# Paired norm transposes, one store per tile, smaller V and q arrays, and a new plan for the front of a two-layer attention and gated-MLP kernel

## The chip, the cores and the metric

The kernel runs on one core of a Trainium2 chip. The metric is device time in microseconds (us) from the first to the last instruction of the core, as the median of several runs. The core has a matmul engine (TensorE, PE in the profile), two engines for elementwise work (VectorE or DVE, ScalarE or ACT), GpSimd (POOL), and SyncE (SP), which here only issues DMAs.

## The reference

Two layers follow each other, with the same weights in both. Each is a sliding-window attention and then a gated MLP, both on a normalised x and both added to x. Everything is bf16; x has 2048 rows of 512.

```python
def _A_ref(x, wqkv, wo):
    H = 32; Dh = D // H; W = 256                      # 32 heads of 16
    q, k, v = ...                                     # x @ wqkv, split
    scores = einsum("bhqd,bhkd->bhqk", q, k) * (Dh ** -0.5)
    mask = (i - j >= 0) & (i - j < W)                 # 256 keys back
    p = softmax(where(mask, scores, -1e9))
    return einsum("bhqk,bhkd->bhqd", p, v) ... @ wo

def _B_ref(x, w_gate, w_up, w_down):                  # 512 -> 1792 -> 512
    return (sigmoid(x @ w_gate) * (x @ w_up)) @ w_down

x = x + _A_ref(_layernorm(x), wqkv, wo)
x = x + _B_ref(_layernorm(x), w_gate, w_up, w_down)
x = x + _A_ref(_layernorm(x), wqkv, wo)
x = x + _B_ref(_layernorm(x), w_gate, w_up, w_down)
```

## The kernel before

The 2048 rows are 16 tiles of 128, in four groups of four. The kernel's Python holds a plan: a small model of the chip (`Plan`) in which engines, queues and transfers have durations. While the program is built, the plan walks through time and decides at each step which unit of matmul work comes next; the other engines take tasks by priority. So the order of every engine's instructions is fixed before the kernel runs, by the plan's constants. Work of the MLP (gate, up, down) fills PE between pieces of attention: scores ("visits", 154 of them, each with one exponential on ScalarE) and values (P times V).

Layer norm of one tile: statistics on VectorE, the root on GpSimd, normalising on VectorE, and then a transpose, since the matmuls need the transposed tile `xnT`. The first eight tiles of layer 0 and two others are transposed by PE, all others by DMA, a tile at a time:

```python
def stats(e):
    nc.vector.bn_stats(out=st[:, 0:6], in_=self.xsb[:, t, :])
    nc.vector.bn_aggr(out=st[:, 6:8], in_=st[:, 0:6])
def root(e):
    nc.gpsimd.tensor_scalar(...); nc.gpsimd.tensor_tensor(..., op=ALU.pow)
def apply(e):                      # takes one of 3 xn buffers
    nc.vector.tensor_scalar(out=b[0][:], in0=self.xsb[:, t, :], ...)

a = pl.task({"DVE": 910}, stats, deps, prio, lambda: self.has("st"))
b = pl.task({"POOL": 800}, root, [a.done], prio)
c = pl.task({"DVE": 406}, apply, [b.done], prio, can, port=True)
if key[:2] == ("p", 0) and t < 8 or key[0] == "g" and self.by_pe(key[1], t):
    ...                            # nc.tensor.transpose x4, then a copy
else:
    d = pl.dma(1210, 131072, lambda: nc.sync.dma_start_transpose(
        out=self.xnT[key][0][:, :, o:o + P], in_=box["xn"][0][:]), [c.done], prio)
```

Buffers, the stores at the end of layer 1, the loads and the warm-up:

```python
self.qT = big.tile([P, NCQ, S], BF16, name="qT")
self.Vaug = [big.tile([P, NBG, VW], BF16, name=f"Vaug{i}") for i in range(3)]   # NBG = 4 tiles each
ring("xn", 3, [P, D]); ring("xnT", 3, [P, KT, TGW]); ring("st", 6, [P, 10], F32)
...
dst = self.out[0, t * P:(t + 1) * P, :].rearrange("(z k) d -> z k d", z=2)
for z in range(2):
    pl.dma(450, HP * D * 2, lambda z=z: nc.sync.dma_start(out=dst[z], in_=self.xsb[z:P:2, t, :]), [d.done])
...
for i in range(0, FC, 2):          # loads of w_down, after wq, wo, gate and up
    parts.append(load(self.wd[:, h, :], wd_src[:, h, :], 2 * P * D * 2, after=at))
    at += gap
...
def matmul(self, mode, ns):        # in the plan
    if self.now < COLD:            # COLD = 13600
        ns *= 2
...
def keep_warm(self, bank):         # when PE would have nothing to do, before 85 us
    for i in range(4):
        nc.tensor.matmul(self.banks[bank][:, 0:P], lhsT=self.ident[:], rhs=self.ident[:], start=True, stop=True)
```

Attention's result goes through two further DMA transposes per tile (OTs to Oq, On to OnT), and halves of V are copied by DMA (Vaug to Vl and Vh). All of these, the norm transposes and the stores are issued by SyncE, in one order.

Of the kernel before, what the change touches and what calls it, by code (L numbers as in the profile page):

```python
# [10 lines left out]
ALU = mybir.AluOpType  # L11
# [18 lines left out]
HP = P // 2  # L30

# [65 lines left out]
PACE = (2700, 3100)  # L97
OVERLAP = {"ACT": 114, "DVE": 83, "POOL": 45, "SP": 0}
LATENCY = {"ACT": 45, "DVE": 40, "POOL": 60, "SP": 0}
EXTRA = {"ACT": 40, "DVE": 10, "POOL": 30, "SP": 70}  # L100
PE_LATENCY = 180
COLD = 13600
SWITCH = 96
DMA_LATENCY = 1500
FETCH = (1200, 1300)
# [62 lines left out]
class Plan:  # L168
# [3 lines left out]
    def __init__(self):  # L172
        self.now = 0.0
        self.heap = []
        self.seq = 0
        self.free = {e: 0.0 for e in OVERLAP}
        self.queue = {e: [] for e in OVERLAP}
        self.mode = None
        self.pe_free = 0.0
        self.dma_free = 0.0  # L180
        self.issued = 0
        self.fetched = -1e9
        self.port_free = 0.0
# [18 lines left out]
    def dispatch(self):  # L202
        moved = True
        while moved:
            moved = False
            for e in ("ACT", "DVE", "POOL", "SP"):
# [4 lines left out]
                for t in q:  # L211
                    if t.port and self.port_free > self.now + 50:
                        continue
                    if not t.began and (t.can is None or t.can()) and (best is None or (t.prio, t.seq) < (best.prio, best.seq)):
                        if len(t.engines) > 1 and self.elsewhere(t, e):
                            continue
                        best = t
# [11 lines left out]
    def begin(self, t, e):  # L229
# [9 lines left out]
        if t.transfer:  # L239
            t.ends = max(t.ends, self.dma_free) + DMA_LATENCY  # L240
            self.at(t.ends, lambda: self.land(t, self.free[e] - 300))
        else:
            self.at(t.ends, t.done.fire)

    def land(self, t, since):

        if self.fetched >= since - FETCH[0]:
            self.at(self.fetched + FETCH[0] + FETCH[1], t.done.fire)
        else:
            t.done.fire()  # L250

    def count(self, n):

        if (self.issued + 2 * n) // 256 > self.issued // 256:
            self.fetched = self.now
            if self.free["SP"] > self.now:
                self.free["SP"] += 900
                self.at(self.free["SP"])
        self.issued += 2 * n

    def dma(self, ns, nbytes, fn, deps=(), prio=5, after=0, queue="SP"):
        def go(e):
            fn()
            self.dma_free = max(self.dma_free, self.now + ns) + nbytes / 250.0

        t = self.task({queue: ns}, go, deps, prio, None, after)
        t.transfer = True
        return t
# [14 lines left out]
    def matmul(self, mode, ns):  # L283
# [3 lines left out]
        if self.mode != mode:  # L287
            ns += SWITCH
            self.mode = mode
        self.pe_free = self.now + ns  # L290
# [8 lines left out]
class Net:  # L299


    def __init__(self, ctx, tc, A_x, wqkv, wo, w_gate, w_up, w_down, out):
# [22 lines left out]
        self.qT = big.tile([P, NCQ, S], BF16, name="qT")  # L325
        self.kTp = [big.tile([P, NCQ, NBG, 2, P], BF16, name=f"kTp{i}") for i in range(2)]
        self.Vaug = [big.tile([P, NBG, VW], BF16, name=f"Vaug{i}") for i in range(3)]
# [10 lines left out]
        self.nhalf = big.tile([P, 1], F32, name="nhalf")  # L338
        self.rms = [big.tile([P, 1], F32, name=f"rm{e}") for e in range(2)]
        self.bufs = {}  # L340

# [3 lines left out]
        ring("xn", 3, [P, D])  # L345
        ring("xnT", 3, [P, KT, TGW])
# [7 lines left out]
        ring("st", 6, [P, 10], F32)  # L354
# [19 lines left out]
    def loads(self, A_x, wqkv, wo, w_gate, w_up, w_down):  # L374
# [8 lines left out]
        def load_x(dst, tiles, n, prio, queues=("SP", "SP"), after=0):  # L383
            done, parts = Event(), []
            for z in range(2):
                src = A_x[0].rearrange("(t z k) d -> z k t d", z=2, k=HP)[z][:, tiles, :]
                parts.append(load(dst[z:P:2], src, n * HP * D * 2, after, (), prio, queues[z]))
# [3 lines left out]
        def load(dst, src, nbytes, after=0, deps=(), prio=2, queue="SP"):  # L391
            ns = max(520, 40 + nbytes / 1024 * 0.95)
            q = {"SP": nc.sync, "ACT": nc.scalar}[queue]
            return pl.dma(ns, nbytes, lambda: q.dma_start(out=dst, in_=src), deps, prio, after, queue).done
# [3 lines left out]
        for i, k in enumerate("kqv"):  # L398
            h = slice("qkv".index(k) * D, ("qkv".index(k) + 1) * D)
            self.has_wq[k] = load(self.wq[:, :, h], wq_src[:, :, h], D * D * 2, prio=0, queue="ACT" if i < 3 else "SP")  # L400

        def x_group(g, after):
            h = slice(g * NBG, (g + 1) * NBG)
            ev = load_x(self.xsb[:, h, :], h, NBG, 2 if g > 1 else 2, after=after)
            for t in range(g * NBG, (g + 1) * NBG):
                self.has_x[t] = ev

        x_group(1, 0)
        gap, at = 1600, 6000
        self.has_wo = load(self.wot[:], wo_src, D * D * 2, after=at)  # L410
        at += gap * 2
        n = F // 2
        gu = []
        for i in range(2):
            h = slice(i * n, (i + 1) * n)
            pair = []
            for w, src in ((self.wg, wg_src), (self.wu, wu_src)):
                pair.append(load(w[:, :, h], src[:, :, h], D * n * 2, after=at))
                at += gap * 7 // 2
            gu.append(pair)  # L420
            if i == 0:
                x_group(2, at)
                at += gap * 2
        self.has_gu = [gu[fc * 2 // FC] for fc in range(FC)]
        self.has_wd = Event()
        parts = []
        for i in range(0, FC, 2):
            h = slice(i, i + 2)
            parts.append(load(self.wd[:, h, :], wd_src[:, h, :], 2 * P * D * 2, after=at))
            at += gap  # L430
        when_all(parts, self.has_wd.fire)
        x_group(3, at)

    def constants(self):
# [4 lines left out]
                                base=0, pattern=[[-1, P]], channel_multiplier=1)  # L439
        nc.vector.memset(self.rms[0][:], 0.0)  # L440
# [4 lines left out]
        n = VS * H // 2  # L445
        for z in range(2):
            eng = nc.vector if z == 0 else nc.gpsimd
            for V in self.Vd[z]:
                eng.memset(V[0:HP, :, n:VW], 0.0)
                eng.memset(V[HP:P, :, 0:n], 0.0)  # L450
                eng.memset(V[HP:P, :, 2 * n:VW], 0.0)
        for V in self.Vaug:
            nc.vector.memset(V[:, :, 0:VS * H].rearrange("p t (h c) -> p t h c", c=VS)[:, :, :, 16:VS], 1.0)
            nc.vector.memset(V[:, :, VS * H:VW], 0.0)
        self.pl.free["POOL"] = 4000.0
# [3 lines left out]
        self.pl.free["DVE"] = 3200.0  # L459

    def later_constants(self):
        nc, pl = self.nc, self.pl

# [20 lines left out]
        a = pl.task({"POOL": 900}, mask, prio=7, port=True)  # L484
# [4 lines left out]
    def layer_norm(self, key, t, deps, prio):  # L489

        nc, pl = self.nc, self.pl
        done = self.xn_ready[key, t]
        box = {}

        def stats(e):
            box["st"] = b = self.take("st")
            st = b[0]
# [3 lines left out]
        def root(e):  # L501
            st = box["st"][0]
            nc.gpsimd.tensor_scalar(out=st[:, 9:10], in0=st[:, 7:8], scalar1=1e-5, scalar2=None, op0=ALU.add)  # L503
            nc.gpsimd.tensor_tensor(out=st[:, 8:9], in0=st[:, 9:10], in1=self.nhalf[:], op=ALU.pow)  # L504
# [10 lines left out]
        def apply(e):  # L515
            box["xn"] = b = self.take("xn")
            if key not in self.xnT:
                self.xnT[key] = self.take("xnT")
            st = box["st"][0]
            nc.vector.tensor_scalar(out=b[0][:], in0=self.xsb[:, t, :], scalar1=st[:, 6:7], scalar2=st[:, 8:9],  # L520
                                    op0=ALU.subtract, op1=ALU.mult)

        a = pl.task({"DVE": 910}, stats, deps, prio, lambda: self.has("st"))
        b = pl.task({"POOL": 800}, root, [a.done], prio)
        c = pl.task({"DVE": 406}, apply, [b.done], prio, can, port=True)
        c.done.then(lambda: self.give(box["st"]))
        o = (t % NBG) * P
        if key[:2] == ("p", 0) and t < 8 or key[0] == "g" and self.by_pe(key[1], t):
            def steps(bank):
                pt = self.tp_view(bank)  # L530
                xn = box["xn"][0]
# [3 lines left out]
            def evac(u):  # L535
                pt = self.tp_view(u.bank)
                d = pl.task({"ACT": act_ns(KT * P), "DVE": dve_ns(KT * P) + 100}, lambda e: self.copy(
                    e, self.xnT[key][0][:, :, o:o + P], pt), [u.done], 0 if t < NBG else 2)
# [4 lines left out]
        else:  # L543
            d = pl.dma(1210, 131072, lambda: nc.sync.dma_start_transpose(
                out=self.xnT[key][0][:, :, o:o + P], in_=box["xn"][0][:]), [c.done], prio)
            d.done.then(lambda: (self.give(box["xn"]), done.fire()))
# [11 lines left out]

    def used(self, key, n):
# [4 lines left out]
    def q_unit(self, L, g, cq):  # L564
        nc, pl, key = self.nc, self.pl, ("p", L, g)
        t0 = g * NBG

        by_tile = L == g == 0 and cq < 1
        w = P if by_tile else TGW

        def steps(bank):
            return [(mm_ns(w), lambda kt=kt, o=o: nc.tensor.matmul(  # L572
                self.banks[bank][:, o:o + w], lhsT=self.wq[:, kt, cq * P:cq * P + P], rhs=self.xnT[key][0][:, kt, o:o + w],
                start=kt == 0, stop=kt == KT - 1)) for o in range(0, TGW, w) for kt in range(KT)]

        def evac(u):
            u.done.then(lambda: self.used(key, 1))
            d = pl.task({"ACT": act_ns(TGW), "DVE": dve_ns(TGW)}, lambda e: self.copy(
                e, self.qT[:, cq, t0 * P:t0 * P + TGW].rearrange("p (t z k) -> p t z k", z=2, k=HP),
                self.banks[u.bank][:].rearrange("p (t k z) -> p t z k", z=2, k=HP)), [u.done], 3)  # L580
# [5 lines left out]
        if L == 1:  # L586
            needs.append(self.seen[0, t0 + NBG - 1])
# [5 lines left out]
    def k_unit(self, L, g, cq):  # L593
# [3 lines left out]
        by_tile = L == g == 0 and cq < 1  # L597
        w = P if by_tile else TGW

        def steps(bank):  # L600
            return [(mm_ns(w), lambda kt=kt, o=o: nc.tensor.matmul(  # L601
                self.banks[bank][:, o:o + w], lhsT=self.wq[:, kt, D + cq * P:D + cq * P + P], rhs=self.xnT[key][0][:, kt, o:o + w],
                start=kt == 0, stop=kt == KT - 1)) for o in range(0, TGW, w) for kt in range(KT)]

        def evac(u):
# [12 lines left out]
            a = pl.task({"ACT": act_ns(TGW), "DVE": dve_ns(TGW)}, cp, [u.done], 3, lambda: self.has("kt"))  # L618
            b = pl.task({"DVE": 620}, split, [a.done], 3, port=True)
# [726 lines left out]
```

The softmax here doesn't subtract the row's maximum and nothing guards it: scores larger than these inputs give would overflow.

## Time and profile before

| | |
|---|---|
| median of 3 runs | 551.94 us (550.83 to 552.82) |
| span of the profiled run | 551.2 us |
| TensorE busy | 527.5 us |
| VectorE busy | 414.5 us |
| ScalarE busy | 395.5 us, of which the 154 exponentials 282.6 |
| GpSimd busy | 63.1 us |
| mean granted clock of TensorE | 0.997 |
| DMA packets | 97,015, 36.41 MB |

In the profile an instruction is named by line, engine and "out<-in". L532 is the transpose by PE, L544 the norm's transpose by DMA, L572, L601 and L637 the projections to q, k and v, L662 gate and up, L695 down, L723 the output projection, L853 to L873 scores, L905 the exponential, L932 values, L1112 the warm-up. "issue" is time in which an engine waited for nothing that the profile shows.

### The profile page before, as it was taken

To read this page: it belongs to the slowest core of one execution; us is meant where nothing else is said; L and a number is where in the kernel's file an instruction comes from. 1 tells how busy PE (TensorE), PEld (TensorE's weight loads), DVE (VectorE), ACT (ScalarE), POOL (GpSimd) and SP (SyncE) were. 2 spreads that over 40 slices of the span, in tenths; PEclk is the share of its full clock that TensorE was granted. 3 is DMA by queue.
4 is the path that set the end of the run, shared out by engine and by line. 5 is a ranking of instruction groups with operands and counts; after the bars stand their busy time and mean duration, and the time that the engine had idled before them with its cause. 6 is when DMAs were issued, how large, how long until landed. Compare 5 with 4: busy or idle time off the path is not lost.

```text
span 551.2 us, 24123 instructions
## 1 busy us (share of the span) xinstructions
PE 527.5 (96%) x10851; PEld 354.7 (64%) x10944; DVE 414.5 (75%) x906; ACT 395.5 (72%) x459; POOL 63.1 (11%) x145
## 2 busy tenths in 40 slices
PE   7998999999999999989999999999999999999996
PEld 6546857756657656656566765666656666767874
DVE  6997889788799799679677696868767677756432
ACT  3897878888888887657587877868788776742321
POOL 5221110110011120002110021000100000000000
PEclk8999999999999999999999999999999999999999
DMA  8694412322334332214401143022541332122000
GB/s 276 209 170 147 51 39 56 65 44 63 46 52 75 64 40 58 45 32 98 70 6 37 42 89 62 12 51 61 96 62 23 40 81 60 41 50 59 21 21 29
DMA packets 97015, 36.41 MB, mean 66 GB/s; under 512 B 79248, under 2 KB 96912, under 8 KB 96912
## 3 DMA queue, kind: packets, MB, share of 16 engines
q1 hardware_dynamic: 95040, 33.04, 30.1%
q8 instruction: 85, 1.39, 1.1%
q10 hardware_dynamic: 1872, 1.84, 1.1%
q14 instruction: 18, 0.15, 0.1%
HBM read 9.70 MB, written 2.10 MB: 21 GB/s over the span
## 4 chain that ended last, share of the span: by engine, by line
PE 87%; DVE 4%; DMA 4%; issue 3%; ACT 1%; POOL 0%; DVEq 0%; ACTq 0%
PE bank L662 33%; PE bank L695 16%; PE bank L932 8%; PE Sps L853 7%; PE bank L723 5%; PE bank L572 5%; PE bank L637 5%; PE bank L601 5%; PE Sps L863 2%; DMA xnT<-xn 2%; DMA OnT<-On 1%; ACT PTring L905 1%; DVE st L498 1%; PE bank L532 1%; DMA out_dram<-xsb 1%
## 5 line engine op out<-in xcount | busy, mean ns | idle before, releaser
L905 ACT ACTIVATE PTring<-Sps 128x2048 bf16<-128x2048 f32 (+1 forms) x122 | 225.9, 1851 | 55.2 <-PE Sps L853 52.3
L662 PE MATMUL bank<-xnT,wg 128*128 128x256 bf16 (+1 forms) x1064 | 140.6, 256 | 0.1
L662 PE MATMUL bank<-xnT,wu 128*128 128x256 bf16 (+1 forms) x1064 | 140.5, 256 | 0.0
L674 ACT ACTIVATE th<-bank 128x256 bf16<-128x256 f32 x224 | 80.2, 384 | 47.9 <-PE bank L662 42.4
L677 DVE SCALAR_TENSOR_TENSOR hT<-th,bank 128x256 bf16<-128x256 bf16 x224 | 87.5, 414 | 30.8 <-ACT th L674 29.8
L695 PE MATMUL bank<-wd,hT 128*128 128x512 bf16 x402 | 103.6, 379 | 2.5 <-issue 1.0
L662 PEld LDWEIGHTS <-wg 128*128 128x128 bf16 x1064 | 88.5, 98 | 23.5 <-issue 1.7
L662 PEld LDWEIGHTS <-wu 128*128 128x128 bf16 x1064 | 90.9, 98 | 12.3 <-issue 0.9
L503 POOL TENSOR_SCALAR st<-st 128x1 f32<-128x1 f32 x64 | 18.6, 291 | 442.4 <-DVE st L499 442.4
L905 ACT ACTIVATE edge<-Sps 128x2048 bf16<-128x2048 f32 (+1 forms) x32 | 56.7, 1773 | 16.8 <-PE Sps L863 16.1
L791 DVE TENSOR_TENSOR PTring<-PTring,mask 128x1024 bf16<-128x1024 bf16 x64 | 44.0, 687 | 30.8 <-ACT PTring L905 30.7
L695 PEld LDWEIGHTS <-hT 128*128 128x128 bf16 x448 | 41.8, 98 | 37.8 <-issue 0.8
L932 PE MATMUL bank<-PTring,Vaug 128*32 128x64 bf16 (+1 forms) x2880 | 52.1, 203 | 3.6 <-issue 3.5
L932 PEld LDWEIGHTS <-Vaug 128*32 128x32 bf16 x2880 | 44.0, 97 | 13.7 <-issue 10.6
L555 DVE CAST OTs<-bank 128x512 bf16<-128x512 f32 x54 | 39.2, 728 | 15.1 <-PE bank L932 14.7
L853 PE MATMUL Sps<-qT,kTp 32*128 32x64 bf16 (+3 forms) x1856 | 47.8, 218 | 1.4 <-ACT PTring L905 0.3
L853 PEld LDWEIGHTS <-kTp 32*128 32x128 bf16 x1856 | 24.5, 92 | 36.7 <-issue 35.0
L932 PE MATMUL bank<-edge,Vl 128*32 128x64 bf16 x1024 | 44.5, 193 | 0.0
L498 DVE BATCH_NORM_STATS2 st<-xsb 128x6 f32<-128x512 bf16 x64 | 43.7, 683 | 0.4
L791 DVE TENSOR_TENSOR edge<-edge,maske 128x1024 bf16<-128x1024 bf16 x60 | 40.8, 682 | 3.3 <-ACT edge L905 3.2
L504 POOL TENSOR_TENSOR st<-st,nhalf 128x1 f32<-128x1 f32 x64 | 40.9, 640 | 5.3
L932 PE MATMUL bank<-edge,Vh 128*32 128x64 bf16 x896 | 40.8, 193 | 0.0
(72 smaller groups left out, 527.1 us busy)
## 6 DMA issues: line engine op xcount, KB each, us to landing
Vl<-Vaug SPq DMA_DIRECT2D x32, 68.0 KB, 2.2
out_dram<-xsb SPq DMA_DIRECT2D x32, 64.0 KB, 1.9
Vh<-Vaug SPq DMA_DIRECT2D x28, 68.0 KB, 2.3
wg<-in_B_w_gate_dram SPq DMA_DIRECT2D x2, 896.0 KB, 11.6
wu<-in_B_w_up_dram SPq DMA_DIRECT2D x2, 896.0 KB, 9.5
wd<-in_B_w_down_dram SPq DMA_DIRECT2D x7, 256.0 KB, 4.4
wq<-in_A_wqkv_dram ACTq DMA_DIRECT2D x3, 512.0 KB, 8.0
xsb<-in_A_x_dram SPq DMA_DIRECT2D x6, 256.0 KB, 6.4
```

Of the source, the lines that this page charges most:

```text
L498: nc.vector.bn_stats(out=st[:, 0:6], in_=self.xsb[:, t, :])
L504: nc.gpsimd.tensor_tensor(out=st[:, 8:9], in0=st[:, 9:10], in1=self.nhalf[:], op=ALU.pow)
L555: self.nc.vector.tensor_copy(out=out, in_=in_)
L572: return [(mm_ns(w), lambda kt=kt, o=o: nc.tensor.matmul(self.banks[bank][:, o:o + w], lhsT=self.wq[:, kt, cq * P:cq * P + P], rhs=self.xn ...
L662: return [(mm_ns(w), lambda i=i, j=j, fc=fc, wt=wt, kt=kt: nc.tensor.matmul(pt[:, i, j, :], lhsT=wt[:, kt, fc * P:(fc + 1) * P], rhs=self. ...
L674: nc.scalar.activation(out=box["th"][0][:], in_=pt[:, 0, :], func=AF.Tanh, scale=0.5)
L677: nc.vector.scalar_tensor_tensor(out=self.hT[:, chunk, :], in0=box["th"][0][:], scalar=1.0, in1=pt[:, 1, :], op0=ALU.add, op1=ALU.mult)
L695: nc.tensor.matmul(self.banks[bank][:], lhsT=self.hT[:, c, o:o + P], rhs=self.wd[:, fc, :], start=fc == 0, stop=fc == FC - 1)
L791: done = pl.task({"DVE": dve_bf_ns(1024)}, lambda e: nc.vector.tensor_tensor(out=r, in0=r, in1=m.to_broadcast([P, 16, HP]), op=ALU.mult), ...
L853: nc.tensor.matmul(self.sps[:, m, o:o + n * HP], lhsT=kTp[32 * m:32 * m + 32, i, tt, e, :], rhs=self.qT[32 * m:32 * m + 32, i, q0:q0 + n * ...
L905: nc.scalar.activation(out=out, in_=src, func=AF.Exp, scale=scale)
L932: nc.tensor.matmul(o, lhsT=Va[:, c0:c0 + 32], rhs=p(h), start=k == 0 or t == 0, stop=k == len(parts) - 1 or t == 0, tile_position=(0, 32 * g))
```

## The change

It has five parts.

- Norms in pairs: except for tiles transposed by PE, two neighbouring tiles share a statistics buffer, one root step on GpSimd, one normalising task and one DMA transpose of 128 by 1024. `xnT` is now laid out by tile, so that a pair is contiguous.
- One store per output tile: the target is read in the order of partitions, so that one DMA of 128 KB takes the place of two.
- V in six arrays of a pair of tiles instead of three of four tiles, so that they come free sooner; q in a ring of three groups instead of all four, which saves memory.
- The constants at the start are cleared mostly by GpSimd instead of VectorE, and partly after the first norms; weight loads are split over two queues, and w_down is loaded later.
- The plan's model of DMA landing and of instruction fetching is new, and its priorities are a table by kind of task, one set for the first 22 visits (the front) and one for the rest.

It is meant to make the start shorter, to keep transfers from coming late, and to spare DMA issues. The matmuls of the reference are the same in number and size, except that runs of scores are cut where the ring of q wraps.

The diff, cut to its core:

```diff
-PACE = (2700, 3100)
+PACE = [2621, 3006, 2091, 2676, 22]
+EARLY = 12
+FILL = 800
-COLD = 13600
+COLD = 5200
-DMA_LATENCY = 1500
-FETCH = (1200, 1300)
+LAND = 1230
+RATE = (280.0, 345.0)
+LANES = 8
+LEAD = (65, 40)
+LINE_NS = 3550
+FETCH = (1200, 2300)
+PRIO = dict(st_x0=8.84, ap_x0=5.2, xt_x0=4.11, st_x1=6.83, ap_x1=4.97, ...)
+RANK = dict(tp=-0.355, o=1.872, lead=10.494, far=6.876, v=1.959, g=2.363, d=3.317, feed=15.682, x3=44361,
+    wd=380, go=211)
+LATE_PRIO = dict(st_p=4.07, ap_p=5, xt_p=3.41, ...)
 ...
-        self.qT = big.tile([P, NCQ, S], BF16, name="qT")
+        self.qT = big.tile([P, NCQ, QG * TGW], BF16, name="qT")
-        self.Vaug = [big.tile([P, NBG, VW], BF16, name=f"Vaug{i}") for i in range(3)]
+        self.Vaug = [big.tile([P, 2, VW], BF16, name=f"Vaug{i}") for i in range(VP)]
-        ring("xn", 3, [P, D])
-        ring("xnT", 3, [P, KT, TGW])
+        ring("xn", 2, [P, 2, D])
+        ring("xnT", 3, [P, NBG, KT, P])
-        ring("st", 6, [P, 10], F32)
+        ring("st", 5, [P, 2, 10], F32)
 ...
+            for w in "kq":
+                h = slice("qk".index(w) * D, ("qk".index(w) + 1) * D)
+                self.has_wq[w] = both([load(self.wq[:, k:k + 2, h], ..., prio=0, queue=q)
+                                       for k, q in ((0, "ACT"), (2, "SP"))])
 ...
+        at = RANK["x3"]
+        x_group(3, at)
         for i in range(0, FC, 2):
-            parts.append(load(self.wd[:, h, :], wd_src[:, h, :], 2 * P * D * 2, after=at))
-            at += gap
+            parts.append(load(self.wd[:, h, :], wd_src[:, h, :], 2 * P * D * 2, after=at + 2 * RANK["wd"] * i))
 ...
-            d = pl.dma(1210, 131072, lambda: nc.sync.dma_start_transpose(
-                out=self.xnT[key][0][:, :, o:o + P], in_=box["xn"][0][:]), [c.done], prio)
+            d = pl.dma(1240, 262144, lambda: nc.sync.dma_start_transpose(
+                out=self.xnT[key][0][:, i:i + 2].rearrange("p t c q -> p (t c) q"),
+                in_=box["xn"][0][:].rearrange("p t d -> p (t d)")), [c.done], self.prio["xt_" + kind], ...)
 ...
-                dst = self.out[0, t * P:(t + 1) * P, :].rearrange("(z k) d -> z k d", z=2)
-                for z in range(2):
-                    pl.dma(450, HP * D * 2, lambda z=z: nc.sync.dma_start(out=dst[z], in_=self.xsb[z:P:2, t, :]), [d.done])
+                dst = self.out[0, t * P:(t + 1) * P, :].rearrange("(z k) d -> k z d", z=2)
+                pl.dma(640, P * D * 2, lambda: nc.sync.dma_start(out=dst, in_=self.xsb[:, t, :]), [d.done], self.prio["out"], base=1340)
 ...
+    @property
+    def prio(self):
+        return PRIO if self.slot < PACE[4] else Late(LATE_PRIO)
```

## The prediction

> **What bounds the kernel now.** I read the page's busy table first, then the engines' busy time by stretches, then the order of PE's instructions at the start, then the chain that ended last, and last the times to landing of the DMAs.
>
> The page of the kernel before, its head, the share of each engine and the chain by engine:
>
> ```profile
> span 551.2 us, 24123 instructions
> ...
> PE 527.5 (96%) x10851; PEld 354.7 (64%) x10944; DVE 414.5 (75%) x906; ACT 395.5 (72%) x459; POOL 63.1 (11%) x145
> ...
> PE 87%; DVE 4%; DMA 4%; issue 3%; ACT 1%; POOL 0%; DVEq 0%; ACTq 0%
> ```
>
> TensorE (PE) carries 87% of the chain and leaves only 551.2 - 527.5 = 23.7 us of the span idle. The change takes no matmul of the reference away, so it can win only from these 23.7 us and from busy time that is slower than need be. Where they lie is shown by the busy time by stretches (start:end, length, then PE busy, and after POOL the granted clock):
>
> ```profile
> 0.00:10.00 10.00, 6.59 (x72) 6.40 (x73) 7.22 (x36) 2.25 (x4) 7.08 (x25) 0.93 0.76 243
> 10.00:20.00 10.00, 9.79 (x120) 6.29 (x121) 7.02 (x22) 8.05 (x12) 2.50 (x6) 0.90 1.07 368
> 40.00:50.00 10.00, 7.97 (x201) 4.85 (x200) 6.57 (x13) 7.21 (x8) 1.13 (x2) 1.00 0.81 195
> 200.00:250.00 50.00, 46.90 (x1081) 29.87 (x1092) 39.90 (x82) 34.46 (x39) 3.46 (x8) 1.00 0.25 44
> 540.00:552.00 12.00, 7.02 (x40) 3.28 (x38) 2.82 (x5) 0.51 (x2) 0.00 (x0) 0.97 0.10 33
> ```
>
> Length minus PE busy, over all stretches that I asked for: 3.4 us in the first ten, 2.0 from 40 to 50, 0.9 from 70 to 80, 0.9 in the rest of the first hundred; 12.0 between 100 and 500, the largest piece 3.1 from 200 to 250; 0.3 from 500 to 540; 4.2 at the end, where the last output tile is added and stored. The clock of 0.93 and 0.90 means half speed over (1-0.93)*10/0.5 = 1.4 us and (1-0.90)*10/0.5 = 2.0 us, 3.4 in all. That is a loss inside busy time.
>
> PE's instructions in order of time (start, duration, instruction, idle before it):
>
> ```profile
> 1.44 5.03 PE L1112 MATMUL bank<-ident 128*128 128x128 bf16 x56 [1.44 <-POOL ident L438]
> 8.44 1.42 PE L532 MATMUL bank<-ident,xn 128*128 128x128 bf16 x12 [1.96 <-DVE xn L520]
> 14.00 0.41 PE L853 MATMUL Sps<-qT,kTp 32*128 32x128 bf16 x24
> 42.83 1.02 PE L572 MATMUL bank<-xnT,wq 128*128 128x512 bf16 x4 [1.97 <-DMA xnT<-xn]
> ```
>
> The 56 matmuls of the warm-up end at 6.47, 2 us before the first transposes. The first scores come at 14.00. At 40.9 PE waits 2 us for a transpose by DMA. The chain that ended last, in order of time (start, duration, what), shows the same hole and others of its kind:
>
> ```profile
> 37.47 5.23 DMA xnT<-xn
> 71.81 3.97 DMA OnT<-On
> 194.88 4.21 DMA OnT<-On
> 233.39 2.32 issue
> 265.79 4.52 DMA xnT<-xn
> 494.88 1.16 issue
> ```
>
> And the issues of DMAs on the page (count, size, median us to landing):
>
> ```profile
> xnT<-xn SPq DMA_TRANSPOSE x54, 2.5
> Oq<-OTs SPq DMA_TRANSPOSE x30, 3.3
> out_dram<-xsb SPq DMA_DIRECT2D x32, 64.0 KB, 1.9
> ```
>
> A transpose that lands in 2.5 us at the median took 4 to 5.2 us wherever it ended on the chain. So the waits are those of late transfers, not of usual ones.
>
> **What the Trainium skill says.** "TensorE: Matmul & The Clock Gate", section "What's actually happening": the clock is halved after an idle window of 3,413 ns and comes back after a busy one. The trace agrees: its half-speed time sums to 3.4 us, one such window, and it follows the idle PE after the warm-up, though that idle time was only 2 us. "Runtime: NRT & Kernel Launch", section "Instruction fetch mechanics": instructions come in blocks of 256 (16 KiB) by DMA and the cost is mostly hidden. Here 85 packets carry 1.39 MB on the instruction queue, 16 KiB each. The waits named "issue" at 233.4 and 494.9, with 152 short matmuls in 1.4 us ahead of the first, suggest that it is not always hidden. "DMA: Bandwidth & Descriptors", section "Issuing engines are not separate DMA queues": queues of different engines share the same 16 DMA engines, so a second queue saves only issue time. For the split weight load at the start I therefore count no more than issue time.
>
> **The change, part by part.**
>
> *Start.* Before, statistics of all four tiles (0.82 us each, from 4.83 to 8.08) run ahead of the first normalisation, and VectorE was still clearing constants at 4.8. In the change most of the clearing goes to GpSimd, and the priorities put normalising (5.2) ahead of further statistics (8.84; the lower goes first). Four tiles need 4 x (0.82 + 0.35) = 4.7 us of VectorE; from about 4.1 that ends at 8.8, where the fourth normalisation before ended near 10.6. So scores could start near 12, 2 us before 14.00. The plan also counts warm-up matmuls at full clock after 5.2 us instead of 13.6, so about 70 are issued instead of 56 (four at a time, 448 ns each four in the plan to 5.2, then 224 ns until the first transposes); that covers the gap and should keep the clock from being halved. Half of the 3.4 us at half speed is real loss (1.7). The two gains overlap, because PE also waits for copies there: I count 2.5 us for both.
>
> *The hole at 40.9.* The loads of the down weights (7 of 256 KB) were issued at 36.3 to 42.4, around the transpose that took 5.23. They now begin near 44 and are spaced by 1.5 us. I count 2.0 of the 2.0 us gone, and 0.7 of the 1.8 us in the rest of the front.
>
> *Transposes in pairs.* Of the 54 norm transposes by DMA, 8 + 14 in layer 0 and 16 + 16 in layer 1, none is left alone: 27 pairs. A pair has the size of Oq, which is issued in 1.26 us (median) against 1.22 for a single one, and lands after 3.3 instead of 2.5. So the SyncE queue loses 27 x 1.22 - 27 x 0.04 = 32 us of issuing, nearly all of it off the chain. In exchange the first tile of a pair waits for the second. Gate and up take two tiles at a time except for the first four and last two, so little waits; on GpSimd the 64 root pairs (0.29 + 0.64 us) become fewer, also off the chain.
>
> *Stores.* 32 become 16, 16 x 0.58 = 9.3 us less of issuing before a longer issue of one is counted. Only the last is on the path: one store after the last addition instead of two in turn, about 0.5 us.
>
> *V in pair arrays, q in a ring.* Same number of V rows (12 tiles), less room for q; runs of scores are cut where the ring wraps, a few more short matmuls: +0.2 us.
>
> *Plan between 100 and 500.* Of the 12.0 us idle I count 3.5 recovered: fewer transfers to be late, and a plan that counts instruction fetches. This is the softest term; a new order may bring new late transfers.
>
> Sum: -2.5 - 2.0 - 0.7 - 3.5 - 0.5 + 0.2 = -9.0 us. From the median of 551.94 that makes 542.9; I say 542.5.
>
> **Rivals.**
>
> *Nothing arrives at the end.* ACT's chain of 154 exponentials, 226 + 57 us, might set the pace, so that a faster front only makes PE wait later. Against it: the last attention is done near 500, and after that PE has 40 us of gate, up and down with 0.3 us idle. Work pushed aside is always at hand. If it were so: 549 to 552.
>
> *New waits in place of the old.* Both tiles of a pair must have been normalised, an xn ring of two pairs instead of three tiles stops a normalisation, and seven scattered weight loads meet V copies. For it: transposes that end on the chain are already 1.5 to 2.7 us late. Against it: PE has gate and up in stock from 60 us on. This would make 548 to 556.
>
> *Nearly all holes closed.* If the new plan meets the chip exactly, some 8 of the 12 us and 6 of the front go: 536 to 538.
>
> **Range and chances.** The front is fairly sure (5 us, give or take 1.5), the middle is not (0 to 8 won, or a few lost). So 542.5, 8 times in 10 between 533 and 551. The limit for over 2% faster is 551.94 x 0.98 = 540.9, only 1.6 below my number: 0.38. Within 2%: 0.56. Over 2% slower needs 11 us of new waits on an engine that had 24: 0.06.
>
> **What would show it.** Clock 1.00 or nearly so in the first 20 us; first scores near 12; no wait for xnT near 41; 27 xnT transposes with a median near 3.3 us; PE idle between 100 and 500 near 8.5 us; 3.7 at the end. I am wrong if that idle time is over 12 us, or if the matmuls themselves (warm-up left out) take longer in busy time, which would mean more switches between forms of matmul.

## Result, and the profile after

The changed kernel takes 545.91 us (median of 4 runs, 545.38 to 546.21) against 552.38 for the kernel before in the same session: a ratio of 0.9897, 95% interval 0.9874 to 0.9920. Run again as a control beside other runs it gave 0.9870 (0.9847 to 0.9893). So 5.7 to 7.2 us are won, 1.0 to 1.3%. The forecast was 542.5, within 533 to 551.

The page of the changed kernel, the same parts as before:

```profile
span 544.5 us, 24319 instructions
...
PE 534.5 (98%) x11068; PEld 354.8 (65%) x11068; DVE 420.6 (77%) x902; ACT 394.5 (72%) x455; POOL 45.3 (8%) x105
...
PE 91%; DVE 3%; DMA 3%; ACT 2%; issue 1%; POOL 0%; ACTq 0%; POOLq 0%
```

PE seems 7 us busier although it has the same work. Compare the counts: here 11,068 matmuls and as many weight loads; before, 10,851 matmuls and 10,944 weight loads. The trace of before lacks 93 matmul records, all of 512-wide matmuls (L695 shows 402 of 448). So part of the "23.7 us idle" on which the forecast stood was missing records.

The busy time by stretches (start:end, length, PE, weight loads, VectorE, ScalarE, GpSimd, granted clock, DMA share, GB/s):

```profile
0.00:10.00 10.00, 8.55 (x109) 8.56 (x110) 5.75 (x24) 2.87 (x4) 6.31 (x25) 1.00 0.75 243
10.00:20.00 10.00, 9.77 (x113) 5.24 (x111) 9.64 (x25) 8.20 (x12) 5.26 (x21) 1.00 1.06 385
40.00:50.00 10.00, 9.98 (x247) 6.61 (x245) 8.83 (x18) 9.09 (x12) 0.81 (x2) 1.00 0.22 71
200.00:250.00 50.00, 50.00 (x1122) 30.98 (x1119) 44.60 (x96) 39.09 (x46) 4.21 (x6) 1.00 0.37 69
540.00:545.00 5.00, 0.69 (x4) 0.10 (x1) 0.69 (x1) 0.00 (x0) 0.00 (x0) 1.00 0.09 29
```

There is no half clock from 10 to 20 any more (before: 0.90), the hole at 40 is gone, and PE shows no gap from 200 to 250. The 1.00 of the first line needs a reading of its own: the record of the clock begins at 6.67 us here and at 5.11 before. Up to there four matmuls of the warm-up take 0.43 us, behind it 0.22, so in both kernels the start runs at half speed.

PE in order of time, at the start and at one new gap:

```profile
1.45 6.22 PE L1265 MATMUL bank<-ident 128*128 128x128 bf16 x64 [1.45 <-POOL ident L536]
7.50 0.39 PE L657 MATMUL bank<-ident,xn 128*128 128x128 bf16 x4
13.29 0.41 PE L1002 MATMUL Sps<-qT,kTp 32*128 32x128 bf16 x24
54.27 0.41 PE L1002 MATMUL Sps<-qT,kTp 32*128 32x192 bf16 x16 [0.82 <-ACT PTring L1055]
```

The warm-up now meets the first transposes, which come 0.9 us earlier; the first scores come at 13.29 instead of 14.00. PE's waits (who <- whom, us in sum, times, longest):

```profile
PE Sps L1002 <- ACT PTring L1055: 2.0, 3, 0.8
PE bank L805 <- DMA xnT<-xn: 0.8, 2, 0.7
```

The first is new. It is 2.0 us in all, at 25, 54 and 95 us; before it was

```profile
PE Sps L853 <- ACT PTring L905: 0.3, 1, 0.3
```

Late transfers still stand on the chain, but PE mostly has other work by then:

```profile
92.49 3.06 DMA xnT<-xn
117.13 4.30 DMA xnT<-xn
180.66 4.79 DMA xnT<-xn
```

And the DMA issues, to be read against those of before (2.5 us for a norm transpose, 1.9 for a store):

```profile
out_dram<-xsb SPq DMA_DIRECT2D x16, 128.0 KB, 2.1
xnT<-xn SPq DMA_TRANSPOSE x27, 3.3
```

**A measure that the missing records don't touch.** Weight loads are complete in both traces, and each is followed by one matmul. From start to start within a run of equal matmuls the trace has 216 ns for 512 columns, 109 for 256, 56 for 128; scores and values run four at a time. All matmuls at these rates are 482.6 us before and 482.4 after (gate and up 196.5, down 96.7, projections 110.5, scores and values 70.4, transposes and warm-up 8.3 to 8.5). What the time from load to load is above that, by stretch:

| us | before | after | control run of after |
|---|---|---|---|
| 0 to 20 | 6.0 | 3.1 | 3.2 |
| 20 to 40 | 1.7 | 2.7 | 2.7 |
| 40 to 50 | 3.4 | 1.3 | 1.3 |
| 50 to 100 | 5.7 | 8.8 | 8.2 |
| 100 to 200 | 12.9 | 13.7 | 13.3 |
| 200 to 300 | 12.8 | 10.0 | 10.4 |
| 300 to the end of matmuls | 20.1 | 16.9 | 16.2 |
| sum | 62.6 | 56.5 | 55.3 |

About 41 us of each sum are the 380 (after: 378) changes between ordinary matmuls, scores and values at about 0.11 us each (a 512-wide matmul ahead of scores takes 0.31 to the next start, not 0.22). They lie a little earlier in the changed kernel, whose attention ends sooner. With 0.108 us for each change taken out, the first hundred is 9.3 before and 7.8 after; 100 to 500 is 12.5 and 7.9. So the first hundred won 1.5 us, the middle 4.6, and the tail from the last addition's end to the end of the span 0.3 (3.4 to 3.1).

Two cautions. The table counts matmuls of the warm-up as work, though they do none. Before, 60 of them ran in the first 20 us and 28 later, up to 86 us; now all 84 run before 11 us. At 0.056 us each and counted as lost, the first 20 us lose 9.4 before and 7.8 after, so the start won 1.6 us and not 2.9. From 20 to 40 and 50 to 100 together the loss goes from 9.0 to 11.5. The whole front then won 1.7 us. And each column is one execution: the changed kernel and its control have the same instructions, and the control is 1.2 us ahead at the last matmul, all of it won between 70 and 350 us.

### The profile page after: what moved, and what is told of

Read it like the earlier page. It is cut to its first block, busy times and chain, and to the rows that moved or that the text cites. A ratio compares the mean times of both kernels' runs of the same rounds, so it can differ in the third digit from the quotient of the medians.

```text
span 544.5 us, 24319 instructions
## 1 busy us (share of the span) xinstructions
PE 534.5 (98%) x11068; PEld 354.8 (65%) x11068; DVE 420.6 (77%) x902; ACT 394.5 (72%) x455; POOL 45.3 (8%) x105
## 4 chain that ended last, share of the span: by engine, by line
PE 91%; DVE 3%; DMA 3%; ACT 2%; issue 1%; POOL 0%; ACTq 0%; POOLq 0%
PE bank L805 35%; PE bank L838 17%; PE bank L1082 9%; PE Sps L1002 7%; PE bank L865 5%; PE bank L713 5%; PE bank L742 5%; PE bank L778 4%; DMA xnT<-xn 2%; PE Sps L1013 2%; PE bank L1265 1%; ACT PTring L1055 1%; ACT edge L1055 1%; DVE edge L933 1%; DMA OnT<-On 1%
## 5 line engine op out<-in xcount | busy, mean ns | idle before, releaser
L805 PE MATMUL bank<-xnT,wg 128*128 128x256 bf16 (+1 forms) x1064 | 138.1, 256 | 1.4 <-DMA xnT<-xn 0.8
L805 PE MATMUL bank<-xnT,wu 128*128 128x256 bf16 (+1 forms) x1064 | 139.1, 256 | 0.0
L838 PE MATMUL bank<-wd,hT 128*128 128x512 bf16 x448 | 115.3, 380 | 0.0
L1055 ACT ACTIVATE edge<-Sps 128x2048 bf16<-128x2048 f32 (+1 forms) x32 | 56.7, 1772 | 12.9 <-PE Sps L1013 12.9
L1002 PEld LDWEIGHTS <-kTp 32*128 32x128 bf16 x1984 | 25.6, 93 | 41.0 <-issue 39.2
L621 POOL TENSOR_SCALAR st<-st 128x2 f32<-128x2 f32 (+1 forms) x37 | 11.2, 303 | 431.6 <-DVE st L616 431.6
L681 DVE CAST OTs<-bank 128x512 bf16<-128x512 f32 x51 | 37.1, 729 | 9.0 <-PE bank L1082 8.8
L933 DVE TENSOR_TENSOR PTring<-PTring,maskn 128x1024 bf16<-128x1024 bf16 x56 | 38.1, 682 | 0.7 <-ACT PTring L1055 0.7
(71 smaller groups left out, 527.5 us busy)
## 6 DMA issues: line engine op xcount, KB each, us to landing
wu<-in_B_w_up_dram SPq DMA_DIRECT2D x2, 896.0 KB, 12.8
```

The lines of the kernel that those rows point to most:

```text
L681: self.nc.vector.tensor_copy(out=out, in_=in_)
L805: return [(mm_ns(w), lambda i=i, j=j, fc=fc, wt=wt, kt=kt: nc.tensor.matmul(pt[:, i, j, :], lhsT=wt[:, kt, fc * P:(fc + 1) * P], rhs=self. ...
L838: nc.tensor.matmul(self.banks[bank][:], lhsT=self.hT[:, c, o:o + P], rhs=self.wd[:, fc, :], start=fc == 0, stop=fc == FC - 1)
L933: done = pl.task({"DVE": dve_bf_ns(1024)}, lambda e: nc.vector.tensor_tensor(out=r, in0=r, in1=m.to_broadcast([P, 16, HP]), op=ALU.mult), ...
L1002: nc.tensor.matmul(self.sps[:, m, o:o + n * HP], lhsT=kTp[32 * m:32 * m + 32, i, tt, e, :], rhs=self.qT[32 * m:32 * m + 32, i, q0:q0 + n * ...
L1055: nc.scalar.activation(out=out, in_=src, func=AF.Exp, scale=scale)
```

## Experiments

Theory at the outset: the new order on PE makes the gain in the middle, the start and the moved loads that of the front, and new waits in the front give some back. Rival: fewer transfers make it. Each run is given as a ratio to the kernel before on its own chip. To compare with the changed kernel I take 0.988 for it (the mean of its two ratios) in the first and third set, and 0.987 in the second, where it ran beside; 0.001 is 0.55 us.

**Pairs issued as singles, nothing else moved.**

```diff
-  lambda: nc.sync.dma_start_transpose(out=self.xnT[key][0][:, i:i + 2]..., in_=box["xn"][0][:]...)
+  lambda: [nc.sync.dma_start_transpose(out=self.xnT[key][0][:, i + k], in_=box["xn"][0][:, k]) for k in range(2)]
```

Expected: 

> The changed kernel, with each of the 27 pair transposes issued as two transposes of one tile at the same place; the order of every engine is otherwise the same. If the new order on PE makes the gain between 100 and 500 us (my theory), the time is within 1 us of the changed kernel, 545.4 to 547. If the gain comes from fewer and therefore less late transfers (rival), 3 to 5 us of it go: 549 to 551, with waits of PE for xnT of more than 3 us in sum.

Measured: 1.0311 (1.0282 to 1.0340), some 24 us slower than the changed kernel, beyond both numbers. PE's waits:

```profile
PE bank L712 <- DMA xnT<-xn: 6.4, 2, 3.6
PE bank L864 <- DMA OnT<-On: 6.2, 5, 2.9
PE bank L804 <- DMA xnT<-xn: 1.9, 2, 1.5
```

All issues of transfers by SyncE took 224 us here and 182 in the changed kernel (231 in the kernel before). 27 further issues of 1.2 us, in a queue that works in order and carries Oq and OnT too, push later transfers past the moment at which PE needs them: so I read the waits; no run shows the two steps apart. The waits also cost clock: four times it was halved for 3.4 us (at 209, 260, 329 and 400 us), at most 4 x 1.7 = 6.8 us of the loss. That the kernel before lived with 54 singles suggests that its order had been made for them. The theory's number fell; but with the order held, this shows what a plan loses on this chip when a queue runs late, not what pairs are worth.

**Warm-up cut to 44.**

```diff
+        self.warmed = getattr(self, "warmed", 0) + 4
-        for i in range(4):
+        for i in range(0 if 44 < self.warmed <= 64 else 4):
             nc.tensor.matmul(self.banks[bank][:, 0:P], lhsT=self.ident[:], ...)
```

Expected: 

> The changed kernel without the last 20 matmuls of the warm-up ahead of the first transposes, all else in the same order. If keeping the clock up is worth what I took for it, the clock of the first 20 us falls below 0.95 and the time rises by 1.2 to 1.7 us, to about 547.4. If PE waits for copies there anyway (rival), it rises by less than 0.4 us although the clock falls.

Measured: 0.9968 (0.9946 to 0.9991), 4.9 us slower than the changed kernel. In the profiled run the clock stayed at 1.00. Instead the third tile's statistics waited for x:

```profile
7.60 0.69 DVE L615 BATCH_NORM_STATS2 st<-xsb 128x6 f32<-128x512 bf16 x1 [1.90 <-DMA xsb<-in_A_x_dram]
8.87 0.40 PE L657 MATMUL bank<-ident,xn 128*128 128x128 bf16 x4 [2.54 <-DVE xn L640]
```

Since the changed order puts the third tile's statistics ahead of the first normalisation, a late x holds all back (in the changed kernel those statistics began at 5.46). The missing matmuls need not be the reason: the run with singles, whose first 10 us are those of the changed kernel, had x late too, began these statistics at 6.20 and was 1.5 us behind at 10 us (0.8 of it a wait for weights). So this run doesn't isolate the clock, and it is inconclusive. The clock does fall more often without the 20 matmuls: its mean was 0.997 in four of the six runs, which fits one stretch of 3.4 us at half speed, and 0.999 or 1.0 in all eight of the changed kernel.

As the order is the same, each matmul can be compared with its twin in the changed kernel. They are 1.7 us behind from 14 us on, and 3.7 more are lost between 80 us and the end, in steps of under 1 us, with 2.0 us of waits for OnT. Why, is not shown: in the run with singles a start that was late by 1.5 us had shrunk to 0.8 at 100 us.

**Loads of the down weights back among the transposes.**

```diff
+ # all seven w_down loads, right behind the first pair transpose; their old places left empty
+ for i in range(0, FC, 2):
+     self.nc.sync.dma_start(out=self.wd[:, i:i + 2, :], in_=src[:, i:i + 2, :])
```

Expected: 

> The changed kernel with all seven loads of the down weights issued right behind the first pair transpose (near 31 us) instead of one by one from 38 us on; PE, DVE, ACT and POOL keep their order. If the loads around the transposes made the hole at 41 us in the kernel before (my theory), the second pair lands over 5 us after its issue, PE waits about 2 us for xnT near 40, and the time is about 548. If the new order has slack there (rival), PE does not wait and the time stays at 546.

Measured: 0.9989 (0.9964 to 1.0014), 6.0 us slower than the changed kernel. The chain, PE's longest wait, and the stretch from 40 to 50:

```profile
34.63 6.62 DMA xnT<-xn
```

```profile
PE bank L722 <- DMA xnT<-xn: 3.7, 1, 3.7
```

```profile
40.00:50.00 10.00, 8.55 (x117) 3.73 (x118) 5.85 (x11) 4.05 (x5) 0.81 (x2) 0.83 0.23 67
```

The second pair lands 6.6 us after its issue, PE waits 3.7, and the idle time halves the clock for a while (0.83 in that stretch). Matmul by matmul, this run is level with the changed kernel up to 35 us, 5.4 us behind at 42 and 5.1 at the end. This one place is all that it lost: 3.7 us of waiting, and 1.7 for the 3.4 us at half clock behind it (42.6 to 46.0). The theory holds, with a larger size.

**The kernel before with three parts and its own order.**

```diff
-        for i in range(4):                                   # warm-up
+        for i in range(5 if self.pl.now < 8000 else 4):
-   # w_down loads between the transposes of tiles 8 to 11
+   # all seven behind the last load of x
-   for z in range(2): dma_start(out=dst[z], in_=self.xsb[z:P:2, t, :])
+   dma_start(out=one, in_=self.xsb[:, t, :])                # one store per tile
```

Expected: 

> The kernel before with three things alone and no new plan: 70 instead of 56 matmuls of warm-up, the loads of the down weights behind the last load of x, one store per output tile. The order of PE, DVE, ACT and POOL is that of the kernel before. If what the front wins is kept to the end, as it must be where PE is the bound (my theory), the three are worth 1.2 to 1.7, 2.0 and 0.5 us: 548.0 to 548.5. If later waits take it back (rival), the time is over 550.5.

Measured: 0.9943 (0.9910 to 0.9977), 3.2 us faster than the kernel before (1.3 to 5.0), where 3.4 to 3.9 was expected. The start (two stretches) and a later gap:

```profile
0.00:10.00 10.00, 7.41 (x90) 6.86 (x90) 7.22 (x36) 2.41 (x4) 7.05 (x25) 1.00 0.76 240
10.00:20.00 10.00, 9.02 (x116) 5.39 (x116) 7.22 (x23) 8.09 (x11) 2.49 (x6) 1.00 1.07 368
```

```profile
51.27 0.38 PE L581 MATMUL bank<-xnT,wq 128*128 128x512 bf16 x1 [1.41 <-issue]
```

The half clock of before (0.93 and 0.90) is gone, but the first scores come at 13.80 instead of 14.00. The order is that of the kernel before, so each matmul can be compared with its twin there. All between 14 and 37 us come 0.2 us earlier: that is what the full clock was worth in this trace, not 1.2 to 1.7. (The first 20 us lose 5.0 instead of 6.0 by the measure of the table, but 0.8 of that is the 14 further matmuls of warm-up.) Matmuls behind the q projection that stood still at 40.9 come 2.3 us earlier. Then the rival sets in: the wait of 1.4 us at 51.3, for nothing that the profile shows, and a smaller one near 65 leave 0.5 us at 70. The other 2.7 us are won after 200 us, mainly near 270 and 497, where the kernel before waited for a transpose and for "issue". The first of these places lies ahead of the first store (363 us), so no moved load, store or warm-up matmul is near it.

In sum this run brings half of what the whole change brings, without any pair, but the trace doesn't show that the three parts are what brings it. Two of the six runs, with a mean clock of 0.996 and 0.997, took 552.8 us and the other four 548.9; where the clock fell in those two is not known.

**Singles, with a plan made for them.**

```diff
+        by_pe = alone; alone = True            # every norm for itself
-        ring("xn", 2, [P, 2, D])
+        ring("xn", 3, [P, 2, D])
```

Expected: 

> The changed kernel with norm transposes of one tile, as in the kernel before (three xn buffers, one root step a tile), planned anew for them, so that the order on all engines differs. If pairs are what took waits away between 100 and 500 us (since the unplanned split cost 25 us), this is 4 to 8 us slower than the changed kernel, 550 to 554, with more waits of PE for xnT and OnT. If a plan made for singles does as well (rival: the 25 us came from a plan that was not made for them), it is within 1.5 us, 545 to 547.5.

Measured: 1.0056 (1.0025 to 1.0087), 10 us slower than the changed kernel, run beside it unaltered as a control. For the control:

> The changed kernel once more, unchanged, beside the next three on one chip: 545 to 548 us, 0.99 of the kernel before. It is there so that the next three are read against it; a ratio over 0.993 would mean that the chip matters as much as the change.

It gave 0.9870. On its face that speaks for pairs. But the values of the priorities had been chosen for pairs, so I searched them for singles too, by small random steps kept when the plan's own end came earlier, and did the same for the pairs. Singles, and then pairs (the first lines of each edit; the other values change likewise):

```diff
 singles
-PACE = [2621, 3006, 2091, 2676, 22]
+PACE = [2621, 3006, 2091, 2985, 22]
-FILL = 800
+FILL = 854
 pairs
-PACE = [2621, 3006, 2091, 2676, 22]
+PACE = [2621, 3006, 2091, 2402, 22]
```

> Norm transposes of one tile each (54 instead of 27), with values of the plan searched in the same way for them. If pairs are needed to keep PE from waiting (what the run with singles and the pairs' values suggests), it is at 549 or more. If the loss of that run lay in values made for pairs and not in the singles (rival), it is at 542 to 546.

> The changed kernel with other values of the plan's priorities, ranks and slacks, found by small random steps that were kept when the plan's own end came earlier; nothing else differs. If the plan's model of DMA landing and instruction fetch is right enough to be followed (my theory), PE waits less in the first 100 us and the time is 542 to 544.5. If such a search only fits the plan's errors (rival), the time is 546 to 549.

Measured: 0.9956 (0.9930 to 0.9982) for singles, 0.9893 (0.9860 to 0.9925) for pairs. (The singles spread widely, from 547.0 to 556.5 us over 22 runs; the ratio leaves out the slowest eight, which count as slow runs, while the six of the pairs lie between 546.7 and 549.7.) The search helped the singles by 5 to 6 us and the pairs not at all on the chip, though it moved the plan's own end in both. Singles remain about 4 us behind, or 5 by the medians of all runs (553.5 and 548.3). So pairs are worth something like 4 us, and the values as much again where they don't fit. With one searched order each, the 4 us are not clear of what another order can do (the last run: 3 us).

**A plan that doesn't know of instruction fetches.**

```diff
+        return 0.0                  # issue(): no fetch is counted, neither for PE nor for DMAs
         late = self.held(n, ns)
```

Expected: 

> The changed kernel with a plan that counts no waits for instruction fetches of PE and no fetches in the way of DMAs; all else as in the change, planned anew. If counting fetches is what took the waits named issue away (3.5 us before, 0.5 after on values), those waits come back with 2 to 4 us: 548 to 550. If not (rival), within 1.5 us of the changed kernel.

Measured: 1.0292 (1.0249 to 1.0335), 23 us slower than the changed kernel. PE's waits, and those of others for the transposes:

```profile
DVE Rt L1137 <- DMA Oq<-OTs: 15.7, 14, 2.8
PEld L866 <- DMA OnT<-On: 8.8, 9, 2.1
PE bank L866 <- DMA OnT<-On: 5.6, 6, 1.6
```

Waits of value matmuls for "issue" are 1.1 us (changed kernel: 0.5), so those 2 to 4 us did not come back; the waits for transfers grew. (The 14.5 us for OnT that the next expectation names are the sum of the second and third line, weight loads and matmuls, which overlap.) So a second plan counted PE's own waits and left out only the landings:

```diff
-            for f in self.fetches[-3:]:        # when a DMA is issued, and when it lands
+            for f in ():
```

Expected: 

> The changed kernel with a plan that counts PE's own waits for instruction fetches but not the DMAs that land later because of a fetch; planned anew. The plan without both was 23 us slower than the change and waited 14.5 us for OnT. If late landings make that loss (my theory), this one is at 560 to 570 too, with over 8 us of waits for OnT and xnT. If PE's own waits make it (rival), it is at 546 to 551.

Measured: 1.0300 (1.0256 to 1.0345), again 23 us behind. PE waits 5.6 us for OnT and 4.9 for xnT, against 0.2 and 0.8 in the changed kernel, and the clock was halved for 13.7 us in all. So a plan that leaves out the late landings loses as much with PE's own waits counted as without. That the landings alone, with PE's waits left out, would save the 23 us was not tried.

**The front's own priorities off.**

```diff
-PACE = [2621, 3006, 2091, 2676, 22]
+PACE = [2621, 3006, 2091, 2676, 0]
```

Expected: 

> The changed kernel with the priorities, paces and ranks of the later part used from the first visit on, so without those of the front. If the front's own priorities are worth what the first 20 us win (my theory), the first scores come 1 to 2 us later, and the time is 547 to 549. If the front's quicker pace costs as much in waits of PE for exponentials as it wins (rival), the time is 545 to 546.5.

Measured: 0.9913 (0.9892 to 0.9934), 2.4 us slower than the changed kernel beside it. That is the number of the theory, but not for its reason. The first exponential starts at 14.4 instead of 13.8, yet the first 20 us lose as much as in the control (8.0 and 7.9, the warm-up counted as lost: 12 more matmuls fill the gap). The loss lies later: 0.9 us from 20 to 40, 0.5 from 50 to 100, 0.8 from 100 to 500.

**What an untuned order costs.**

```diff
-EXP_NS = 1880
+EXP_NS = 1876                       # in the plan of the kernel before; no meaning on the chip
```

Expected: 

> The kernel before with 1876 instead of 1880 ns for an exponential in its plan: no meaning on the chip, only another order. If an order that nobody tuned costs little (theory: the order as such is worth under 2 us), it is within 2 us of the kernel before. If the order as such is worth as much as the whole change (rival), it is 4 to 10 us slower than the kernel before.

Measured: 1.0058 (1.0041 to 1.0076), 3.2 us slower than the kernel before: between the two. This other order alone costs 3 us, half of what the change won. Any run above that planned anew carries an uncertainty of about this size.

## Why the prediction was right in direction, and where it was off

It was right that PE is the bound, that only idle and slow PE time can be won, and that some 1% to 2% would come. It forecast 9.0 us in sum; 6.5 came (552.38 to 545.91). By its own steps:

- *The measure.* "Leaves only 551.2 - 527.5 = 23.7 us of the span idle" took idle time from a trace that lacks 93 matmuls. By weight loads PE lost 62.6 - 41 = 21.6 us between its first and its last matmul, the half clock included, and 12.5 of it between 100 and 500; that the page's 12.0 lies close to it is luck. "PE idle between 100 and 500 near 8.5" failed for that reason: the page after, without missing records, has 1.8, the weight loads 7.9.
- *Start, 2.5 us:* 1.6 came, with the warm-up counted as lost. The half clock behind the warm-up went away as said, but that was worth 0.2 us in the run with three parts, since PE waits for other engines in the same stretch. The step "half of the 3.4 us at half speed is real loss (1.7)" had this wrong. First scores near 12 did not come: 13.29. The fourth normalisation ended at 9.5 and not 8.8; it waited 0.7 us for GpSimd's root, and the warm-up at full speed began at 6.7 us, not at the plan's 5.2 (64 matmuls ran ahead of the first transposes, not 70).
- *The hole at 40.9, 2.0 us:* 2.1 came, and putting the loads back brought it back at 3.7. "They now begin near 44" was wrong, though: three of the seven are issued from 35.1 to 36.3, but behind both pair transposes (29.0 and 32.5), and four from 46.7 on.
- *"0.7 of the 1.8 us in the rest of the front":* this step failed. From 20 to 40 and from 50 to 100 the new plan lost 2.5 us more than the old one, of which 0.6 are six further changes between matmul forms. The largest part that the trace names are the 2.0 us in which PE waits for exponentials: scores are put in before ScalarE is done. My rival "new waits in place of the old" named xn buffers and V copies, but not these. With it the front as a whole won 1.7 us instead of 5.2.
- *Plan between 100 and 500, 3.5 us:* 4.6 came. The landing time of 27 pairs is 3.3 us at the median, as forecast.
- *Stores, 0.5 us:* 0.3 came at the tail.
- *Ring of q:* 128 more score matmuls; the 0.2 us could not be told apart.

The mechanism was right, that PE's waits are what can be won. The front's term was mis-sized by 3.5 us: 0.9 at the start, 2.6 in the rest. That the sum still came near is owed in part to the middle, which brought more than was said of it. How its 4.6 us divide between pairs and the order stays open: pairs are worth about 4 us by the searched runs, an order as such about 3, and the two depend on each other. Part may be chance of one execution: in the run with three parts the same 400 us, with the old order and single transposes, lost only 9.6 us instead of 12.5.

## What to carry to other kernels

In a kernel whose order is fixed ahead, check the plan's landing times of transfers against the trace before tuning anything else: plans that left late landings out lost 23 us here. Move bulk loads away from small transfers that PE waits for (5 us here). Halving the number of small transfers on a queue that works in order seems worth it (about 4 us here, not clear of what another order does). Where two runs have the same order, compare them matmul by matmul; it shows where time is lost and whether a gain is kept. Do not count filler matmuls as work. Before a gap in a profile is called idle, compare the counts of matmuls and weight loads.

## What the runs showed of the hardware that I had not expected

Transposes by DMA landed later where a packet of PE's instruction queue started within 2.4 us after their issue. Medians over all transposes whose landing the trace shows, in the kernel before: OnT 3.53 us with such a packet (10 cases), 2.44 without (17). xnT: 4.13 (18) against 2.48 (32). Oq: 4.36 (7) against 3.22 (19). In the changed kernel it is 3.07 against 2.45, 3.89 against 3.24 and 3.88 against 3.12; in its control 2.92 against 2.43, 3.89 against 3.20 and 3.91 against 3.11. The share that meets a fetch is a third in both kernels; with fewer transposes, 35 such cases became 22. That the fetch is the cause was not tried by itself, but plans that ignore it lose 23 us.

Of 3.4 us at half speed, only 0.2 were won when they went away, because PE waited for other engines in the same stretch. And the length of an idle stretch alone did not decide about the clock: 2.0 us without a matmul (6.47 to 8.44) were followed by half speed from 8.52 to 11.94 in the kernel before, 3.7 us (37.6 to 41.3) in the run with early loads by half speed from 42.6 to 46.0, but 2.5 us (6.3 to 8.9) in the run with 44 matmuls by none. The point at which the warm-up reaches full speed moves as well, from 4.1 to 6.9 us over the traces of the changed kernel and its variants.
